# Two steps of the second phase's weight preparation on GpSimd instead of VectorE

## The chip, the cores and the metric

The kernel runs on one core of one Trainium2 chip. Its time is the device time of one execution in microseconds (us), as the median over several executions. A core has five engines that each work through their own list of instructions in order and wait for each other by semaphores: TensorE (PE in the profile; PEld is its weight load), VectorE (DVE), ScalarE (ACT), GpSimd (POOL) and SyncE (SP), which here only issues transfers (DMA).

## The reference

Three parts follow each other, all in float32:

```
attention, per batch (8) and head (8):   x 512x64, state 32x64
  xread = softmax(x state^T / 8) state            512 rows
  sread = softmax(state x^T / 8) x                 32 rows
  y0 = [xread; sread] of all heads                544 x 512 per batch
first phase, per batch:
  h = relu(y0 w_in)                               512 -> 1024
  c = conv_w[0] h[s-1] + conv_w[1] h[s] + conv_w[2] h[s+1]
  y = (h * sigmoid(c)) w_out                      1024 -> 512
second phase, per batch, y1 the row before:
  xk = mu_k y + (1 - mu_k) y1     xr = mu_r y + (1 - mu_r) y1
  out = sigmoid(xr w_r) * (relu(xk w_k)^2 w_v)
```

w_in, w_out, w_k, w_v and w_r are given as 64-bit floats; the kernel gets their bits as two 32-bit words each.

## The kernel before, in words

**Products.** Matrices are kept as a high and a low part in a format of float32 that TensorE takes; `mm3` (lines 111 to 117) makes a product from three: high by high (line 115), high by low (116) and low by high (117). So nearly every operand needs two steps: a copy to the high part (`hi`, ScalarE) and a subtraction that gives the low part (`lo`, mostly VectorE).

**Weights.** `Weights` (lines 120 to 170) loads and converts a chunk of 128x1024 weights. `load` puts the 64-bit words into a buffer `raw`; `split` makes float32 values and their two parts: ScalarE takes the low words' absolute value into `mid` (line 161) and scales the high words (163); VectorE sets the sign (164), clamps `mid` between two constants (165) and joins both (166); ScalarE copies the high part out (168) and VectorE subtracts (169). `raw` and `mid` have two buffers each (line 20), shared in turn by all chunks, so a chunk's load waits for the low part (169) of the chunk two before it. The second phase has ten chunks: four of w_k, four of w_v and two of w_r.

**Phases.** The first phase goes through nine tiles t: one per batch with 512 tokens (0 to 7; the attention of the next batch runs beside them) and one with the state rows of all batches. Each tile has eight blocks f of 128 inner columns. A block is a product `hps` on TensorE, then `hb` (relu, ScalarE, line 452), `cacc` (the convolution: one step on ScalarE, 468, two on VectorE, 470), `g` (sigmoid on ScalarE, 478, a product on VectorE, 479), `gs` (high part on ScalarE, 485, low part, 487, on GpSimd for tiles 0 to 2 and on VectorE for the others), and the products `acc` of `gs` with w_out, which sum over the blocks. After a tile `yo` goes to memory. GpSimd fills the two border columns of each `hb` (451) and copies two columns to `carry` (453). The second phase loads `y` again as `yt`, forms `mix` and `xk`, `xr` from it (557 to 565), and has blocks of its own: `kps`, `k`, `k2`, `ks`, sums `acc` with w_v, and `rps` with w_r.

**Order.** The code gives every piece of work a priority by its block (lines 750 to 795); the pieces that prepare weights get theirs from `weight_at` (725), some blocks before they are needed. The framework then lays the instructions of each engine into one fixed list by these priorities and by the durations that its own planner assumes. On the chip each engine keeps that list: a step that waits holds back everything behind it on its engine. The first w_k chunk is converted near the end of tile 6 of the first phase.

Of the kernel before, what the change touches and what calls it, by code (L numbers as in the profile page):

```python
# [8 lines left out]
F32 = mybir.dt.float32  # L9
# [3 lines left out]
ALU = mybir.AluOpType  # L13
# [19 lines left out]
def tile_kernel(  # L33
# [26 lines left out]
    nc = tc.nc  # L60
# [11 lines left out]
    N = 512  # L72
# [10 lines left out]
    wp = ctx.enter_context(tc.tile_pool(name="wp", bufs=1))  # L83
    stg = ctx.enter_context(tc.tile_pool(name="stg", bufs=2))
# [3 lines left out]
    op = ctx.enter_context(tc.tile_pool(name="op", bufs=1))  # L88
# [31 lines left out]
    class Weights:  # L120

        def __init__(self, src, many, n, pool, tag="", home=None):
            self.src, self.many, self.n, self.pool, self.tag, self.home = src, many, n, pool, tag, home
            self.wide = src[0].dtype != F32

# [17 lines left out]
        def split(self, w, first=0):  # L145

            hi, lo = w[:, 0], w[:, 1]
            if not self.wide:
                nc.scalar.activation(hi, self.raw, AF.Copy)
                nc.vector.tensor_tensor(lo, self.raw, hi.bitcast(F32), op=ALU.subtract)
                return
            many = w.shape[2]
            raw = self.raw[:, first:first + many]
            v, e = raw[:, :, :, 0], raw[:, :, :, 1]
            x = self.tile([P, many, self.n], U32, "mid")
            vf, ef, xf = v.bitcast(F32), e.bitcast(F32), x.bitcast(F32)  # L160
            nc.scalar.activation(xf, ef, AF.Abs, scale=2.0**16)
            most = float.fromhex("0x1.dffffep+32")
            nc.scalar.activation(v, v, AF.Copy, scale=0.936 * 2.0**-29)
            nc.vector.scalar_tensor_tensor(v, e, 0x80000000, v, op0=ALU.bitwise_and, op1=ALU.bitwise_or)
            nc.vector.tensor_scalar(xf, xf, scalar1=2.0, scalar2=most, op0=ALU.max, op1=ALU.min)
            nc.vector.scalar_tensor_tensor(v, x, 3, v, op0=ALU.logical_shift_left, op1=ALU.bitwise_or)
            return (
                nc.scalar.activation(hi, vf, AF.Copy),
                nc.vector.tensor_tensor(lo, vf, hi.bitcast(F32), op=ALU.subtract),
            )  # L170

    W = {}
# [2 lines left out]

        return tc.issue_after(i.ins)

    def weight(src, key, tag, pool, k, many, group, home=None):


        r = Weights([src[k + i] for i in range(many)], many, N, stg, home=home)

        def split(first=0, n=many):
            g = (key, "group", k // group)
            if k % group == 0 and first == 0:
                W[g] = pool.tile([P, 2, group, N], F32R, tag=f"{tag}{k // group}", name=f"{key}{k}")
            o = k % group + first
            for i in range(n):
                W[key, k + first + i] = W[g][:, :, o + i]
            return r.split(W[g][:, :, o:o + n], first)  # L190

        return r.load, split
# [332 lines left out]
    def load_y(t, pool):  # L525
        q0, ss = tok_segs(t)
        n = ss[-1][2] + ss[-1][1]
        y = pool.tile([P, KC, N + 2], F32, tag="yt", name="yt", bufs=1)
        o = 0
        while o < n:  # L530
            b, s = divmod(q0 + o, T + 1)
            s -= 1
            if s < 0:
                m = 1
                nc.gpsimd.memset(y[:, :, o:o + 1], 0.0)
            elif s < S - 1:
                m = min(n - o, S - 1 - s)
                nc.sync.dma_start(out=y[:, :, o:o + m], in_=y_d[b][:, :, s:s + m])
            else:
                m = min(n - o, T - s)  # L540
                c = b * E + s - (S - 1)
                nc.sync.dma_start(out=y[:, :, o:o + m], in_=y_d[B][:, :, c:c + m])
            o += m
        yt[t] = y
# [84 lines left out]
    def at_half(k, *fns, prio=None):  # L629
        p = 500 * k - AHEAD if prio is None else prio  # L630
        half.setdefault(k, []).extend((fn, p) for fn in fns)

    def run_half(k):
        for fn, p in half.pop(k, []):
            tc.cur_priority = BASE + p
            fn()
# [88 lines left out]
    def weight_at(w, need, at):  # L725
        at_half(at, w[0], w[1], prio=500 * need - WEIGHT_AHEAD)
# [22 lines left out]
    p2 = None  # L749
    for i in range(len(slots) + 2):  # L750
        if i < len(slots):
            ph, t, f = slots[i]
            if (ph, t, f) == (1, B - 1, 2):
                ap_cm.__exit__(None, None, None)
                p2 = ctx.enter_context(tc.tile_pool(name="p2", bufs=1))
                for k in range(0, KF, 2):
                    w = weight(w_k, "k", "wk", p2, k, 2, 2)
                    h = h2 + 2 * k
                    weight_at(w, h, h - 4)
                for k in range(0, KF, 2):  # L760
                    w = weight(w_v, "v", "wa", wp, k, 2, 4)
                    h = h2 + 2 * k + 4
                    weight_at(w, h + 1, h - 3)
                for k in range(0, KC, 2):
                    w = weight(w_r, "r", "wb", wp, k, 2, 2)
                    h = h2 + 8
                    weight_at(w, h, h - 2)
                at_half(2 * i + 4, lambda: load_y(0, p2))
                for c in range(KC):
                    at_half(h2 - 7 + 2 * c, lambda c=c: mix(0, 0, c, p2))  # L770
                    at_half(h2 + 2 + c, lambda c=c: mix(0, 1, c, p2))
            if ph == 2:
                if f == 2 and t + 1 < NT2:
                    at_half(2 * i + 2, lambda t=t: load_y(t + 1, p2))
                    for c in range(KC):
                        at_half(2 * i + 4 + 2 * c, lambda t=t, c=c: mix(t + 1, 0, c, p2))
                if f == 0 and t:
                    for c in range(KC):
                        at_half(2 * i + c, lambda t=t, c=c: mix(t, 1, c, p2))
                if f >= 4 and f - 4 < W2[t] // P:  # L780
                    at_half(2 * i, lambda t=t, f=f: g2_r(t, f - 4))

        def emit(k, d):
            if 0 <= i - d < len(slots):
                ph, t, f = slots[i - d]
                tc.cur_priority = BASE + 1000 * (i - d) + STAGE[k]
                FN[ph][k](t, f)

        emit(0, 0)
        emit(3, 2)  # L790
        emit(2, 1)
        emit(1, 0)
        run_half(2 * i)
        emit(4, 2)
        run_half(2 * i + 1)
# [55 lines left out]
```

## Time and profile before

| | us |
|---|---|
| median of 3 executions | 886.2 (883.36 to 887.11) |
| profiled execution, its own time | 881.77 |
| its span, first to last instruction | 879.9 |
| TensorE busy | 853.5 (97%) |
| VectorE busy | 546.4 (62%) |
| ScalarE busy | 545.6 (62%) |
| GpSimd busy | 105.4 (12%) |
| mean granted TensorE clock | 0.984 of full speed |

The shares are means over stages that differ much. A row of a timeline has the start from the beginning of the span, the duration, the engine, the line of the kernel, the operation, what it writes and reads, and in brackets how long the engine was idle before it and what ended that. Duration and start of neighbouring rows overlap a little, since an engine begins a step before the last one has left it.

### The profile page before, as it was taken

Reading aid. Unit: us, or ns where it says so; the run is one execution under the profiler, and the core shown is the slowest. Engines: PE = TensorE matmul, PEld = TensorE weight load, DVE = VectorE, ACT = ScalarE, POOL = GpSimd, SP = SyncE. Lnnn points to the kernel's source line nnn. Section 1 sums busy time; section 2 is a strip of 40 time slices with the busy share of each in tenths; the row PEclk is TensorE's granted clock in tenths of the full one; section 3 lists DMA queues with packets and bytes.
Section 4 is the critical chain, followed back from the end, with each engine's and each line's share of the span. In section 5 each row is a group of like instructions: output and inputs, shape, how many; then the busy total and the mean of one; then the engine's idle time right before and its main releaser. Section 6 shows DMA issues by size and latency. Waiting matters only on the chain.

```text
span 879.9 us, 11844 instructions
## 1 busy us (share of the span) xinstructions
PE 853.5 (97%) x4406; PEld 686.2 (78%) x4406; DVE 546.4 (62%) x908; ACT 545.6 (62%) x952; POOL 105.4 (12%) x215
## 2 busy tenths in 40 slices
PE   5989999999999997999999999999999999999997
PEld 2557787788778775899888888888888888888886
DVE  6899987899799879999645533425334253332311
ACT  6787875787578658888756645636356364553421
POOL 1144543422111111210000000000000000000000
PEclk7899999999999998999999999999999999999999
DMA  9351254525534364233210211011100111001010
GB/s 340 116 197 49 102 143 128 150 75 160 156 114 121 96 197 151 96 144 120 98 48 37 49 48 31 17 48 49 48 23 26 49 48 48 19 18 48 1 48 36
DMA packets 45512, 76.85 MB, mean 87 GB/s; under 512 B 8336, under 2 KB 30352, under 8 KB 43408
## 3 DMA queue, kind: packets, MB, share of 16 engines
q1 hardware_dynamic: 45456, 76.12, 26.6%
q8 instruction: 34, 0.56, 0.3%
q14 instruction: 22, 0.18, 0.1%
HBM read 45.66 MB, written 17.86 MB: 72 GB/s over the span
## 4 chain that ended last, share of the span: by engine, by line
PE 88%; DVE 5%; ACT 3%; DMA 2%; SPq 1%; issue 1%; DVEq 0%; ACTq 0%
PE acc L115 14%; PE acc L116 14%; PE acc L117 14%; PE kps L115 7%; PE kps L116 7%; PE kps L117 7%; PE rps L117 4%; PE rps L116 4%; PE rps L115 4%; PE hps L115 3%; PE hps L117 3%; PE hps L116 3%; PE p_s L297 2%; PE p_m L116 1%; PE p_m L117 1%; SPq L248 1%
## 5 line engine op out<-in xcount | busy, mean ns | idle before, releaser
L594 DVE TENSOR_TENSOR ks<-k,ks 128x512 fp32r<-128x512 f32 (+1 forms) x72 | 47.6, 662 | 119.8 <-ACT ks L593 119.2
L116 PE MATMUL kps<-xk,k 128*128 128x512 f32 (+1 forms) x288 | 110.1, 382 | 0.0
L115 PE MATMUL kps<-xk,k 128*128 128x512 f32 (+1 forms) x288 | 110.1, 383 | 0.0
L117 PE MATMUL kps<-xk,k 128*128 128x512 f32 (+1 forms) x288 | 110.0, 382 | 0.0
L116 PE MATMUL acc<-gs,out 128*128 128x512 f32 (+1 forms) x288 | 109.6, 382 | 0.0
L117 PE MATMUL acc<-gs,out 128*128 128x512 f32 (+1 forms) x288 | 109.1, 380 | 0.0
L115 PE MATMUL acc<-v,ks 128*128 128x512 f32 x272 | 106.7, 392 | 0.0
L116 PE MATMUL acc<-v,ks 128*128 128x512 f32 x272 | 105.9, 389 | 0.0
L117 PE MATMUL acc<-v,ks 128*128 128x512 f32 x272 | 105.8, 392 | 0.0
L470 DVE SCALAR_TENSOR_TENSOR cacc<-hb,vcol,cacc 128x512 f32<-128x512 f32 (+1 forms) x138 | 103.3, 759 | 3.2 <-ACT cacc L468 2.7
L115 PE MATMUL acc<-gs,out 128*128 128x512 f32 (+1 forms) x288 | 95.0, 391 | 5.8 <-ACT gs L485 5.8
L559 DVE SCALAR_TENSOR_TENSOR mix<-yt,muc,mix 128x384 f32<-128x384 f32 (+7 forms) x128 | 61.4, 500 | 47.0 <-ACT mix L557 46.2
L593 ACT ACTIVATE ks<-k 128x512 fp32r<-128x512 f32 (+1 forms) x72 | 43.5, 605 | 71.2 <-PE acc L117 71.0
L557 ACT ACTIVATE mix<-yt,om 128x384 f32<-128x384 f32 (+7 forms) x128 | 61.5, 516 | 33.0 <-DMA yt<-y 16.2
L580 ACT ACTIVATE k<-kps 128x512 f32<-128x512 f32 (+1 forms) x72 | 40.9, 569 | 50.4 <-PE kps L117 50.0
L115 PEld LDWEIGHTS acc<-gs,out 128*128 128x128 f32 x288 | 54.0, 192 | 18.3 <-ACT gs L485 7.3
L116 PEld LDWEIGHTS acc<-gs,out 128*128 128x128 f32 x288 | 54.2, 188 | 13.1 <-issue 2.5
L565 DVE TENSOR_TENSOR xr<-mix,xr 128x512 fp32r<-128x512 f32 (+1 forms) x36 | 23.8, 661 | 62.8 <-ACT xr L564 62.8
L117 PEld LDWEIGHTS acc<-gs,out 128*128 128x128 f32 x288 | 54.2, 188 | 10.6 <-issue 0.8
L116 PEld LDWEIGHTS kps<-xk,k 128*128 128x128 f32 x288 | 54.4, 189 | 10.4
L117 PEld LDWEIGHTS kps<-xk,k 128*128 128x128 f32 x288 | 54.3, 188 | 10.2
L115 PEld LDWEIGHTS kps<-xk,k 128*128 128x128 f32 x288 | 54.2, 188 | 10.2
(138 smaller groups left out, 1762.1 us busy)
## 6 DMA issues: line engine op xcount, KB each, us to landing
out<-r SPq DMA_DIRECT2D x34, 256.0 KB, 2.0
xT<-x_t SPq DMA_DIRECT2D x32, 256.0 KB, 4.0
xn<-x_n SPq DMA_DIRECT2D x8, 1024.0 KB, 4.9
y<-yo SPq DMA_DIRECT2D x8, 1024.0 KB, 4.3
me<-m SPq DMA_DIRECT2D x48, 128.0 KB, 2.4
m_odd<-m SPq DMA_DIRECT2D x48, 128.0 KB, 2.4
raw<-w_out SPq DMA_DIRECT2D x8, 512.0 KB, 4.7
raw<-w_k SPq DMA_DIRECT2D x8, 512.0 KB, 4.5
```

The source lines that it names most:

```text
L115: nc.tensor.matmul(ps, lh, rh, start=start and k == 0, stop=False)
L116: nc.tensor.matmul(ps, lh, rl, start=False, stop=False)
L117: nc.tensor.matmul(ps, ll, rh, start=False, stop=stop and k == last)
L248: nc.sync.dma_start(out=m_of(b + j, q)[ri, :, g].bitcast(F32), in_=r[rj, :, i].bitcast(F32))
L297: nc.tensor.matmul(self.v["s", g][NS * j:NS * (j + 1), :], sT[self.b][r, h // 2, h % 2], xT[self.b][r, h // 2], start=True, stop=True,)
L470: nc.vector.scalar_tensor_tensor(a[:, :n], hb[:, k:k + n], w[k], a[:, :n], op0=ALU.mult, op1=ALU.add)
L557: nc.scalar.activation(tmp[:, o:o + m], y[:, c, q - 1:q - 1 + m], AF.Copy, scale=om[:, i:i + 1])
L559: nc.vector.scalar_tensor_tensor(tmp[:, o:o + m], y[:, c, q:q + m], muc[:, i:i + 1], tmp[:, o:o + m], op0=ALU.mult, op1=ALU.add,)
L565: nc.vector.tensor_tensor(dst[t][:, 1, c, :n], tmp[:, :n], hi.bitcast(F32), op=ALU.subtract)
L580: nc.scalar.activation(k[:, :n], s["p"][:, :n], AF.Relu)
L593: nc.scalar.activation(ks[:, 0, :n], s["k2"][:, :n], AF.Copy)
L594: nc.vector.tensor_tensor(ks[:, 1, :n], s["k2"][:, :n], ks[:, 0, :n].bitcast(F32), op=ALU.subtract)
```

## The change

For the ten chunks of the second phase, the clamp of `mid` and the subtraction for the low part are issued on GpSimd; the chunks of the first phase keep them on VectorE. `Weights` gets the engine as an argument, and `weight` hands it on. Sizes, buffers, priorities and the arithmetic are as they were. In the changed kernel all lines from 125 on have a number one higher.

```diff
--- before.py
+++ after.py
@@ -121,7 +121,8 @@
 
 
 
-        def __init__(self, src, many, n, pool, tag="", home=None):
+        def __init__(self, src, many, n, pool, tag="", home=None, helper=None):
+            self.helper = helper or nc.vector
             self.src, self.many, self.n, self.pool, self.tag, self.home = src, many, n, pool, tag, home
             self.wide = src[0].dtype != F32
 
@@ -162,11 +163,11 @@
             most = float.fromhex("0x1.dffffep+32")
             nc.scalar.activation(v, v, AF.Copy, scale=0.936 * 2.0**-29)
             nc.vector.scalar_tensor_tensor(v, e, 0x80000000, v, op0=ALU.bitwise_and, op1=ALU.bitwise_or)
-            nc.vector.tensor_scalar(xf, xf, scalar1=2.0, scalar2=most, op0=ALU.max, op1=ALU.min)
+            self.helper.tensor_scalar(xf, xf, scalar1=2.0, scalar2=most, op0=ALU.max, op1=ALU.min)
             nc.vector.scalar_tensor_tensor(v, x, 3, v, op0=ALU.logical_shift_left, op1=ALU.bitwise_or)
             return (
                 nc.scalar.activation(hi, vf, AF.Copy),
-                nc.vector.tensor_tensor(lo, vf, hi.bitcast(F32), op=ALU.subtract),
+                self.helper.tensor_tensor(lo, vf, hi.bitcast(F32), op=ALU.subtract),
             )
 
     W = {}
@@ -175,10 +176,10 @@
 
         return tc.issue_after(i.ins)
 
-    def weight(src, key, tag, pool, k, many, group, home=None):
-
-
-        r = Weights([src[k + i] for i in range(many)], many, N, stg, home=home)
+    def weight(src, key, tag, pool, k, many, group, **how):
+
+
+        r = Weights([src[k + i] for i in range(many)], many, N, stg, **how)
 
         def split(first=0, n=many):
             g = (key, "group", k // group)
@@ -754,15 +755,15 @@
                 ap_cm.__exit__(None, None, None)
                 p2 = ctx.enter_context(tc.tile_pool(name="p2", bufs=1))
                 for k in range(0, KF, 2):
-                    w = weight(w_k, "k", "wk", p2, k, 2, 2)
+                    w = weight(w_k, "k", "wk", p2, k, 2, 2, helper=nc.gpsimd)
                     h = h2 + 2 * k
                     weight_at(w, h, h - 4)
                 for k in range(0, KF, 2):
-                    w = weight(w_v, "v", "wa", wp, k, 2, 4)
+                    w = weight(w_v, "v", "wa", wp, k, 2, 4, helper=nc.gpsimd)
                     h = h2 + 2 * k + 4
                     weight_at(w, h + 1, h - 3)
                 for k in range(0, KC, 2):
-                    w = weight(w_r, "r", "wb", wp, k, 2, 2)
+                    w = weight(w_r, "r", "wb", wp, k, 2, 2, helper=nc.gpsimd)
                     h = h2 + 8
                     weight_at(w, h, h - 2)
                 at_half(2 * i + 4, lambda: load_y(0, p2))
```

The framework orders all engines anew. On ScalarE, at the end of tile 6 (`hb_3361` is block 6 of that tile, `gs_3355` its block 4, `k0_4040` the first chunk of w_k, `mid_4135` and `raw_4131` the second), there stood:

```order
L452 ACTIVATE hb_3361<-hps_3348 128x512
L168 ACTIVATE k0_4040<-raw_4037 128x1024
L478 ACT_TABLE_LOAD
L478 ACTIVATE g_3321<-cacc_3259 128x512
L478 ACTIVATE g_3358<-cacc_3328 128x512
L468 ACTIVATE cacc_3365<-hb_3361,vcol_97 128x512
L161 ACTIVATE mid_4135<-raw_4131 128x1024
L163 ACTIVATE raw_4131<-raw_4131 128x1024
L485 ACTIVATE gs_3355<-g_3321 128x512
```

and there stands now:

```order
L453 ACTIVATE hb_3361<-hps_3348 128x512
L479 ACT_TABLE_LOAD
L479 ACTIVATE g_3321<-cacc_3259 128x512
L469 ACTIVATE cacc_3365<-hb_3361,vcol_97 128x512
L479 ACTIVATE g_3358<-cacc_3328 128x512
L169 ACTIVATE k0_4040<-raw_4037 128x1024
L162 ACTIVATE mid_4135<-raw_4131 128x1024
L164 ACTIVATE raw_4131<-raw_4131 128x1024
L486 ACTIVATE gs_3355<-g_3321 128x512
```

The first chunk's high part has moved from the front of the table load to behind the second `g`; the same eight steps stand between `hb_3361` and `gs_3355`.

On VectorE, at tile 6's last two blocks (`gs_3481` and `gs_3514`; `raw_4131` and `raw_4155` are the second w_k chunk and the first w_v chunk), there stood:

```order
L169 TENSOR_TENSOR k2_4134<-raw_4131,k2_4134 128x1024
L470 SCALAR_TENSOR_TENSOR cacc_3491<-hb_3487,vcol_97,cacc_3491 128x512
L166 SCALAR_TENSOR_TENSOR raw_4155<-mid_4159,raw_4155 128x1024
L487 TENSOR_TENSOR gs_3481<-g_3407,gs_3481 128x512
L479 TENSOR_TENSOR g_3484<-g_3484,hb_3410 128x512
L470 SCALAR_TENSOR_TENSOR cacc_3491<-hb_3487,vcol_97,cacc_3491 128x512
L470 SCALAR_TENSOR_TENSOR cacc_3524<-hb_3520,vcol_97,cacc_3524 128x512
L487 TENSOR_TENSOR gs_3514<-g_3484,gs_3514 128x512
```

and there stands now:

```order
L480 TENSOR_TENSOR g_3407<-g_3407,hb_3361 128x512
L471 SCALAR_TENSOR_TENSOR cacc_3414<-hb_3410,vcol_97,cacc_3414 128x512
L167 SCALAR_TENSOR_TENSOR raw_4131<-mid_4135,raw_4131 128x1024
L488 TENSOR_TENSOR gs_3481<-g_3407,gs_3481 128x512
L165 SCALAR_TENSOR_TENSOR raw_4155<-raw_4155 128x1024
L471 SCALAR_TENSOR_TENSOR cacc_3491<-hb_3487,vcol_97,cacc_3491 128x512
L480 TENSOR_TENSOR g_3484<-g_3484,hb_3410 128x512
L471 SCALAR_TENSOR_TENSOR cacc_3491<-hb_3487,vcol_97,cacc_3491 128x512
L167 SCALAR_TENSOR_TENSOR raw_4155<-mid_4159,raw_4155 128x1024
L471 SCALAR_TENSOR_TENSOR cacc_3524<-hb_3520,vcol_97,cacc_3524 128x512
L488 TENSOR_TENSOR gs_3514<-g_3484,gs_3514 128x512
```

The second w_k chunk's low part (`k2_4134`) is gone from here, and the step of the w_v chunk that reads `mid_4159` has moved from ahead of `gs_3481` to behind it, two places ahead of `gs_3514`.

On GpSimd, over the same stretch, there stood:

```order
L535 MEMSET yt_3641 128x4
L451 MEMSET hb_3410 128x2
L451 MEMSET hb_3487 128x2
L453 COPY carry_100<-hb_3410 128x2
L453 COPY carry_100<-hb_3487 128x2
L451 MEMSET hb_3520 128x2
L453 COPY carry_100<-hb_3520 128x2
L451 MEMSET hb_3563 128x2
```

and there stands now:

```order
L536 MEMSET yt_3641 128x4
L452 MEMSET hb_3410 128x2
L170 TENSOR_TENSOR k0_4040<-raw_4037,k0_4040 128x1024
L166 TENSOR_SCALAR mid_4135<-mid_4135 128x1024
L452 MEMSET hb_3487 128x2
L454 COPY carry_100<-hb_3410 128x2
L452 MEMSET hb_3520 128x2
L454 COPY carry_100<-hb_3487 128x2
L166 TENSOR_SCALAR mid_4159<-mid_4159 128x1024
L454 COPY carry_100<-hb_3520 128x2
L170 TENSOR_TENSOR k2_4134<-raw_4131,k2_4134 128x1024
L452 MEMSET hb_3563 128x2
```

Three clamps (`mid_4135`, `mid_4159` and, further up, the first chunk's) and two low parts (`k0_4040`, `k2_4134`) stand between the fills and copies of `hb`.

On TensorE, at the products of tile 6's last block, there stood:

```order
L115 MATMUL acc0_3181<-gs_3514,out6_716 128x512
L115 MATMUL acc1_3182<-gs_3514,out6_716 128x512
L115 MATMUL acc2_3183<-gs_3514,out6_716 128x512
L115 MATMUL acc3_3184<-gs_3514,out6_716 128x512
L115 MATMUL hps_3620<-aring_102,m_odd_554 128x512
L116 MATMUL hps_3620<-aring_102,m_odd_554 128x512
L117 MATMUL hps_3620<-aring_102,m_odd_554 128x512
L115 MATMUL hps_3620<-aring_102,m_odd_554 128x512
L116 MATMUL hps_3620<-aring_102,m_odd_554 128x512
L117 MATMUL hps_3620<-aring_102,m_odd_554 128x512
L116 MATMUL acc0_3181<-gs_3514,out6_716 128x512
```

and there stands now:

```order
L115 MATMUL acc0_3181<-gs_3514,out6_716 128x512
L115 MATMUL acc1_3182<-gs_3514,out6_716 128x512
L115 MATMUL acc2_3183<-gs_3514,out6_716 128x512
L115 MATMUL acc3_3184<-gs_3514,out6_716 128x512
L116 MATMUL acc0_3181<-gs_3514,out6_716 128x512
L117 MATMUL acc0_3181<-gs_3514,out6_716 128x512
```

The block `hps_3620` of the next tile has moved from between the high products and the low ones to a place behind them all.

## Rows read from the trace of the kernel before

**Rows 1.** Windows: length; busy PE, PEld, DVE, ACT, POOL; clock, DMA share, GB/s.
```profile
80.00:120.00 40.00, 39.91 (x204) 32.10 (x202) 37.97 (x59) 30.03 (x52) 23.82 (x33) 1.00 0.30 99
320.00:340.00 20.00, 12.73 (x109) 9.36 (x108) 17.10 (x26) 17.38 (x25) 2.87 (x8) 0.84 0.68 211
340.00:420.00 80.00, 80.00 (x451) 71.89 (x450) 77.09 (x121) 67.56 (x120) 11.44 (x31) 1.00 0.34 122
420.00:880.00 460.00, 455.27 (x2009) 375.71 (x2007) 171.51 (x294) 231.04 (x427) 0.63 (x6) 1.00 0.12 38
```

**Rows 2.** TensorE's waits: us in total, times, longest us.
```profile
PE acc L115 <- ACT gs L485: 5.8, 2, 5.6
```

**Rows 3.** TensorE's timeline, tile 6 to 7: start, us, line, operation [idle before].
```profile
335.91 2.07 PE L115 MATMUL acc<-gs,out 128*128 128x512 f32 x4 [5.56 <-ACT gs L485]
...
340.34 0.52 PE L115 MATMUL hps<-aring,m_odd 128*128 128x512 f32 x1
...
343.70 1.07 PE L115 MATMUL acc<-gs,out 128*128 128x512 f32 x4
```

**Rows 4.** ScalarE's timeline from the last `hb` before the gap.
```profile
328.03 0.60 ACT L452 ACTIVATE hb<-hps 128x512 f32<-128x512 f32 x1 [2.09 <-PE hps L117]
329.08 1.13 ACT L168 ACTIVATE k<-raw 128x1024 fp32r<-128x1024 f32 x1 [0.45 <-PE p_srT L396]
```

**Rows 5.** VectorE's groups by shape, 340 to 420: count, busy us, mean ns.
```profile
L470 DVE SCALAR_TENSOR_TENSOR cacc<-hb,vcol,cacc 128x512 f32<-128x512 f32 x18 | 13.2, 745 | 0.0
...
L479 DVE TENSOR_TENSOR g<-g,hb 128x512 f32<-128x512 f32 x10 | 6.8, 684 | 0.0
L165 DVE TENSOR_SCALAR mid<-mid 128x1024 f32<-128x1024 f32 x7 | 4.8, 691 | 0.2 <-ACT mid L161 0.2
...
L169 DVE TENSOR_TENSOR k<-raw,k 128x1024 fp32r<-128x1024 f32 x3 | 3.7, 1217 | 0.0
```

**Rows 6.** Lines 487 and 227 on GpSimd: count, shortest/median/longest ns.
```profile
L487 POOL TENSOR_TENSOR gs<-g,gs x24: 1277/1363/1793, 35.9 to 174.2; 128x512 fp32r<-128x512 f32 x24
...
L227 POOL TENSOR_TENSOR aux<-sT,aux x6: 733/831/1717, 69.3 to 181.7; 128x256 fp32r<-128x256 f32 x6
```

**Rows 7.** GpSimd's groups by shape, whole execution.
```profile
L652 POOL MEMSET aux<- 128x2048 f32 x1 | 1.8, 1805 | 0.0
...
L306 POOL MEMSET s<- 128x1 f32 x8 | 0.7, 100 | 7.2 <-DVE sr L387 7.2
masks.py:199 POOL TENSOR_SCALAR_AFFINE_SELECT ident<-ident 128x128 f32<-128x128 f32 x1 | 0.3, 292 | 0.0
```

**Rows 8.** Timelines of VectorE and GpSimd, first tiles.
```profile
79.70 1.78 DVE L470 SCALAR_TENSOR_TENSOR cacc<-hb,vcol,cacc 128x512 f32<-128x512 f32 x1
...
79.26 1.67 POOL L487 TENSOR_TENSOR gs<-g,gs 128x512 fp32r<-128x512 f32 x1 [0.52 <-ACT gs L485]
```

**Rows 9.** VectorE's groups by shape, 80 to 120.
```profile
L470 DVE SCALAR_TENSOR_TENSOR cacc<-hb,vcol,cacc 128x512 f32<-128x512 f32 x17 | 16.3, 969 | 0.6 <-ACT cacc L468 0.4
L479 DVE TENSOR_TENSOR g<-g,hb 128x512 f32<-128x512 f32 x8 | 7.1, 890 | 0.1
```

**Rows 10.** Timelines of VectorE and TensorE, tile 6's last block.
```profile
348.75 0.68 DVE L487 TENSOR_TENSOR gs<-g,gs 128x512 fp32r<-128x512 f32 x1
...
350.50 1.07 PE L115 MATMUL acc<-gs,out 128*128 128x512 f32 x4
...
352.77 0.39 PE L116 MATMUL acc<-gs,out 128*128 128x512 f32 x1
```

**Rows 11.** DMA issues: count, KB each, median us from issue to landing.
```profile
raw<-w_v SPq DMA_DIRECT2D x8, 512.0 KB, 4.6
```

**Rows 12.** Timelines of SyncE's queue, VectorE and TensorE, start of phase two.
```profile
414.36 1.24 SPq L538 DMA_DIRECT2D yt<-y  x2
...
415.34 1.22 DVE L169 TENSOR_TENSOR k<-raw,k 128x1024 fp32r<-128x1024 f32 x1
...
423.37 0.34 PE L117 MATMUL kps<-xk,k 128*128 128x384 f32 x1
```

## Prediction

> **What bounds the kernel now.** The windows by stage come first [rows 1]. From 340 us on TensorE is busy in every microsecond (80.00 of 80, then 455.27 of 460, the rest being the tail), so nothing that another engine saves there can shorten the kernel; another engine can only make TensorE wait. The second view is TensorE's own waits [rows 2]: the longest that the change can touch is 5.6 us on `gs`, made by ScalarE's line 485. In TensorE's timeline it ends at 335.91 [rows 3], near the end of tile 6 of the first phase, exactly where the first weights of the second phase are converted. The fourth view is ScalarE's timeline there [rows 4]: after `hb` at 328.03 it runs the first `k` (329.08) and then a table load, two `g`, a `cacc` and the second chunk's `mid` and `raw` before the `gs` for which TensorE stands still. Last, VectorE between 340 and 420 us: 77.09 us busy in 80 [rows 1]. So TensorE bounds the stretch, with VectorE just behind it.
>
> After that wait TensorE also ran slowly: the granted clock was 0.84 in 320 to 340 [rows 1], four matmuls took 2.07 us at 335.91 and 1.07 us at 343.70, and the slow row ends at 340.34 [rows 3]. That is 1.2 for 2.4 GHz over 4.4 us, so 2.2 us lost. The hole and its slow exit are worth 5.6 + 2.2 = 7.8 us, the most that can be won.
>
> **What the change moves between VectorE and GpSimd.** There are ten chunks of 128x1024. Each takes a clamp of 0.69 us and a low part of 1.22 us from VectorE. Between 340 and 420 that is 7 clamps, 4.8 us, and 8 lows (three of `k`, three of `v` and two of `r`), 9.8 us: 14.6 us off [rows 5].
>
> GpSimd shows neither operation at this size. The low: the same subtraction takes at least 1.28 us there for 128x512 and at least 0.73 for 128x256 [rows 6], so 0.55 us per 256 columns and 1.28 + 1.10 = 2.4 us for 1024 (bounds: 2.3, and 2.7 as twice the median of 1.36). The clamp reads one operand. Bounds: 0.9 us, half the 1.8 us of a fill of 2048 columns that reads nothing, and 2.4 us, as a low. The nearest row is the select of 128 columns, which reads one operand: 0.29 us; less the 0.1 of the smallest fill, 1.5 ns a column, so 1.6 us, which I take [rows 7]. In the stretch GpSimd gains 7 x 1.6 + 8 x 2.4 = 30.4 us.
>
> This is not free for VectorE. At 79.26 a `gs` low began on GpSimd and ended at 80.93; the VectorE step that began at 79.70 took 1.78 us [rows 8] where its kind takes 0.74 [rows 5], and ended 0.55 us after GpSimd did. Over 80 to 120 the same two kinds averaged 969 and 890 ns [rows 9], against 745 and 684 where GpSimd has no such work [rows 5]: 17 x 0.224 + 8 x 0.206 = 5.5 us lost beside 23.8 us of GpSimd [rows 1], 23%. These kinds, with two operands in SBUF, filled 45% of that window. After the change nearly all VectorE work in 340 to 420 is of that sort: (77.1 - 14.6) / 80 = 78%. Scaled, 23% becomes 40%, or 12 us of the 30.4. Net: 14.6 off, 12 back, 2.4 us of relief; bounds 30.4 x 0.23 = 7.0 back (7.6 of relief) and all 30.4 back (15.8 worse). VectorE is hardly relieved, though the new order leans on it as if it were.
>
> The Trainium skill, "SBUF — State Buffer", section "SBUF: two separate sides", speaks against the change: VectorE and GpSimd lock the port pair that they share for a whole instruction, and the loser blocks fully, a VectorE step with two SBUF inputs included when the GpSimd step reads SBUF. The pair of rows agrees. By it all the time that falls over such steps is lost; that is the third rival, priced there from rows.
>
> **The first hole.** ScalarE has the same eight steps between `hb` and `gs`; only the first `k` moves behind the two `g`. In the trace `k` waited 0.45 us before 329.08 [rows 4]; later, it waits no more, provided the clamp and VectorE's step after it are done by 332 (a clamp from 323.3 to 325, then about 4 us of queued VectorE work). So the hole shrinks by 0.45 us; bounds 0 and 7.8 won. `hb` at 328.03 waits for transfers and matmuls that are not moved.
>
> **The place where TensorE will wait.** Tile 6's last block. Its low part ran at 348.75 and TensorE used it at 352.77, after the four high products at 350.50 and a block of `hps` between [rows 10]. The new order has no `hps` there: the low is wanted at about 351.4. On VectorE it now stands behind the step on line 167 that waits for GpSimd's clamp of the first `v` chunk. By hand: the first `k` low runs on GpSimd from 333 to 335.5 and frees the raw buffer, so `v` loads from 335.6, lands 4.6 us later [rows 11], and its `mid` ends at 341.4. The second chunk's clamp has held GpSimd until 342; two small copies and the `v` clamp then get in between VectorE's steps until about 348. Line 167 ends near 350, and the second `k` low, ready since 345, takes 2.4 us about then. One `cacc` and the block's low follow: ready at about 353.7, 2.3 us late. Behind the waiting step stand the next tile's `cacc` and `g`, and behind those ScalarE's `gs`.
>
> The Trainium skill, "GPSIMD Engine Reference", section "Engine selection", has one-input work on GpSimd at roughly line rate; at the 1.2 GHz of its table the clamp would take about 0.9 us, an estimate. Two clamps stand in this place, so it would cost 2.3 - 2 x 0.7 = 0.9 us, and the sum below would be 3.5. No row here shows the operation.
>
> Three more places are alike: the third `k` low (2.4 for 1.2), the two first `v` lows in a row (4.8 for 2.4), and the two `r` lows (4.8 for 2.4). They hold VectorE 1.2 + 2.4 + 2.4 = 6.0 us longer. Of this I count half: TensorE's lead of 3.3 us at 348.75 [rows 10] would hide any one of them, the 1.9 us that is left of it without the `hps` would not hide two.
>
> Sum: -0.45 + 2.3 + 3.0 = +4.9. After 440 nothing is changed: TensorE is full and its matmuls are the same. The profiled execution took 881.77 (span 879.9 and 1.9 around it), so 886.7 now; it lay 4.4 us under the median of 886.2, so **891 us**. Its own range, by the bounds of clamp and lock, is +1 to +11: 887 to 897.
>
> **The rivals.** *Hidden anyway.* In 80 to 120 TensorE was busy 39.91 of 40 us beside 23.8 us of GpSimd [rows 1], so the lock need not reach it; against it, VectorE then had half its work in forms that do not wait. Only the 0.45 remains: 881.3, on the median 886.
>
> *The hole goes.* If `gs` could pass the weights, up to 7.8 us: 874.0, or 878. ScalarE's order speaks against it: `k`, `mid` and `raw` still stand ahead.
>
> *Full lock.* Every GpSimd microsecond over a two-operand step is lost: 30.4 x 0.78 = 23.7, less 14.6, is 9.1; VectorE had 2.9 free, so 6.2 us reach TensorE: 888.0, or 892. It lies inside the forecast's range, and its chance is part of the forecast's.
>
> *The last `k` chunk comes late (slower still).* Its low began at 415.34, was there at 416.56, and TensorE used it at 423.37 [rows 12]: 6.8 us in hand. Each load waits for the low two chunks ahead, now 1 to 3 us later; and the third `v` chunk's second half now loads behind two `yt` transfers, while ScalarE takes that chunk's `mid` and `raw` before this `k`. If `yt` goes out as late as 414.36 for 1.24 us [rows 12]: 415.6, 4.6 to land, 3 x 1.1 on ScalarE, 2.4 for the low make 425.9, so 2.5 us late, and with clamps and contention up to 8. It decides once `yt` goes out after about 412. With the forecast's 4.9: 889 to 895 own, 894 to 899.
>
> **How the numbers follow.** Forecast 0.52 (0.12 of it by the full lock), hidden 0.26, the hole goes 0.10, late last chunk 0.12. A measurement here can tell 0.5%, 4.4 us, from no change; so slower begins at 890.6. Of the forecast 0.30 lie above it; with 0.12, slower is 0.42. Same is 0.22 + 0.26 = 0.48, faster 0.10. The range 882 to 899 leaves out the vanished hole and the far ends of the late cases.
>
> **What would show it.** Right: a TensorE wait of 1 to 3 us near 351 on `gs` from line 488, and more between 355 and 425; VectorE's `cacc` steps above 0.8 us on average in 340 to 420; lows near 2.4 and clamps near 1.6 us on GpSimd; the hole near 330 still at 5 us or more; `v` loading at about 335.6. Wrong: TensorE busy throughout 340 to 420 (hidden), the first hole under 2 us, or the long wait on `k` or `r` after 405.

## The result and the profile after

Four runs each: 895.06 us (892.41 to 897.27) after, 886.21 us (883.36 to 887.11) before. The ratio is 1.0113, with a 95% interval of 1.0081 to 1.0145, so the change made the kernel 0.8 to 1.5% slower. The forecast was 891 us, the range 882 to 899.

The profiled execution took 895.52 us with a span of 893.7, against 881.77 and 879.9. These 13.8 us are 8.1 us more in which TensorE was idle (893.7 - 859.2 busy, against 879.9 - 853.5) and 5.7 us more in which it was busy with the same matmuls, most of it at a lower clock. Not all of this is the change's. Up to about 320 us the two kernels have the same order on all engines, and still the later execution was behind there. This is the last step before the orders part on VectorE, first in the kernel before, then in the changed one:

```profile
321.73 1.23 DVE L164 SCALAR_TENSOR_TENSOR raw<-raw 128x1024 uint32<-128x1024 uint32 x1 [0.34 <-DMA m_odd<-m]
```

```profile
324.74 1.23 DVE L165 SCALAR_TENSOR_TENSOR raw<-raw 128x1024 uint32<-128x1024 uint32 x1 [0.32 <-DMA m_odd<-m]
```

The later execution is 3.0 us behind. So 13.8 - 3.0 = 10.8 us lie behind 320 us, beside the 8.85 between the medians. Two windows behind it, as [rows 1]:

```profile
320.00:340.00 20.00, 12.95 (x118) 9.72 (x117) 13.80 (x21) 15.24 (x23) 8.74 (x8) 0.93 0.61 172
340.00:420.00 80.00, 76.01 (x400) 66.62 (x399) 77.17 (x104) 60.32 (x108) 53.95 (x46) 0.95 0.30 109
```

The row for 340 to 420 tells most of it. GpSimd went from 11.44 to 53.95 us busy and VectorE, which gave work away, is busy 77.17 us where it was 77.09. TensorE, busy in all 80 us before, has gaps of 4 us, and its clock fell. Its waits in 320 to 460, as [rows 2]:

```profile
PE acc L115 <- DVE yo L505: 5.3, 2, 3.2
PE acc L115 <- ACT gs L486: 5.1, 1, 5.1
PE hps L115 <- DMA me<-m: 1.9, 1, 1.9
PE acc L116 <- DVE gs L488: 0.5, 1, 0.5
PE kps L115 <- ACT k L581: 0.3, 1, 0.3
```

and where they end in its timeline, as [rows 3]:

```profile
338.84 2.07 PE L115 MATMUL acc<-gs,out 128*128 128x512 f32 x4 [5.07 <-ACT gs L486]
...
355.21 0.50 PE L116 MATMUL acc<-gs,out 128*128 128x512 f32 x1 [0.50 <-DVE gs L488]
...
398.00 0.40 PE L115 MATMUL acc<-gs,out 128*128 128x272 f32 x1 [3.24 <-DVE yo L505]
...
436.71 0.79 PE L115 MATMUL acc<-v,ks 128*128 128x512 f32 x1 [2.05 <-DVE yo L505]
```

The old hole is still there, 5.07 us for 5.56. New are 0.50 + 3.24 + 0.34 + 2.05 = 6.1 us, of which 5.3 are waits for `yo`: at the end of an output tile VectorE copies every second accumulator out of PSUM, and TensorE can't start the next sum in it before. Net 5.6 us of idle time. The granted clock adds to it. It was at its lower level, 1.2 of 2.4 GHz, about the end of the hole in both kernels, and in the changed one also about the end of each of the two waits for `yo`. First the kernel before, then the changed one, the clock is the third number from the right:

```profile
333.00:341.00 8.00, 5.09 (x13) 4.04 (x14) 7.80 (x12) 8.00 (x13) 1.36 (x4) 0.57 0.35 138
```

```profile
337.00:345.00 8.00, 6.16 (x16) 4.89 (x17) 7.05 (x11) 5.70 (x11) 7.76 (x6) 0.57 0.50 176
398.00:403.00 5.00, 5.00 (x28) 5.00 (x28) 4.96 (x10) 4.61 (x9) 1.96 (x3) 0.66 0.76 302
436.00:440.00 4.00, 3.29 (x9) 2.77 (x10) 2.80 (x4) 1.83 (x3) 2.42 (x1) 0.57 0.64 217
```

The 0.43 of 8 us, 0.34 of 5 and 0.43 of 4 that are missing make 6.8 us, against 0.43 of 8 = 3.4 before, so 3.4 more. 5.6 + 3.4 are 9.0 of the 10.8. Of the rest 0.3 is a longer wait for the last transfer of `me`; 1.5 us are not assigned.

Why the copies came late is seen where two lows stand back to back on GpSimd. GpSimd's row first, then VectorE's:

```profile
390.72 5.04 POOL L170 TENSOR_TENSOR v<-raw,v 128x1024 fp32r<-128x1024 f32 x2 [1.28 <-ACT v L169]
```

```profile
392.03 1.46 DVE L480 TENSOR_TENSOR g<-g,hb 128x286 f32<-128x286 f32 x1 [1.76 <-ACT g L479]
393.42 2.66 DVE L471 SCALAR_TENSOR_TENSOR cacc<-hb,vcol,cacc 128x286 f32<-128x286 f32 x1
396.00 0.54 DVE L566 TENSOR_TENSOR xk<-mix,xk 128x384 fp32r<-128x384 f32 x1
396.47 0.50 DVE L471 SCALAR_TENSOR_TENSOR cacc<-hb,vcol,cacc 128x286 f32<-128x286 f32 x1
396.90 0.44 DVE L488 TENSOR_TENSOR gs<-g,gs 128x286 fp32r<-128x286 f32 x1
397.26 0.68 DVE L505 COPY yo<-acc 128x512 f32<-128x512 f32 x1
```

The first low ends near 393.2, the second at 395.76. The `g` step of 0.45 us took 1.46 and ended just behind the first, the `cacc` step of 0.50 took 2.66 and ended 0.3 us behind the second; between the two VectorE got in one step. The copy could have run from about 392, when TensorE had ended the last product of its sum, and stood behind them until 397.26. With their own durations the same steps in the same order would have let it end near 394.8, an estimate from the rows; TensorE stood still from 394.76 on. So the two lows make this wait. The 1.76 us in which VectorE was idle before, for a `g` of ScalarE, had used up the slack.

The other wait has the same form; GpSimd's row, then VectorE's:

```profile
432.81 2.42 POOL L170 TENSOR_TENSOR k<-raw,k 128x1024 fp32r<-128x1024 f32 x1
```

```profile
432.88 3.42 DVE L167 SCALAR_TENSOR_TENSOR raw<-mid,raw 128x1024 uint32<-128x1024 uint32 x1 [0.74 <-POOL mid L166]
```

The join took 3.42 us for 1.22, and the copy of `yo` started at 436.23. With its own 1.22 the copy would have ended near 434.5, an estimate again; TensorE stood still from 434.66. The clamp has a part in it: the join had waited 0.74 us for `mid`, and without that it would have begun ahead of the low.

VectorE's groups in 340 to 420, as [rows 5]:

```profile
L471 DVE SCALAR_TENSOR_TENSOR cacc<-hb,vcol,cacc 128x512 f32<-128x512 f32 x18 | 17.5, 983 | 0.0
L471 DVE SCALAR_TENSOR_TENSOR cacc<-hb,vcol,cacc 128x286 f32<-128x286 f32 x16 | 13.9, 873 | 0.1
L165 DVE SCALAR_TENSOR_TENSOR raw<-raw 128x1024 uint32<-128x1024 uint32 x6 | 9.2, 1540 | 1.5 <-ACT raw L164 1.5
...
L566 DVE TENSOR_TENSOR xr<-mix,xr 128x384 fp32r<-128x384 f32 x3 | 3.8, 1266 | 0.0
```

In the kernel before, the first took 745 ns [rows 5] and the others:

```profile
L164 DVE SCALAR_TENSOR_TENSOR raw<-raw 128x1024 uint32<-128x1024 uint32 x7 | 8.6, 1225 | 1.2 <-ACT raw L163 1.2
L470 DVE SCALAR_TENSOR_TENSOR cacc<-hb,vcol,cacc 128x286 f32<-128x286 f32 x16 | 8.2, 511 | 0.0
...
L565 DVE TENSOR_TENSOR xr<-mix,xr 128x384 fp32r<-128x384 f32 x4 | 2.2, 552 | 0.0
```

Against these durations the four lost 4.3 + 5.8 + 1.9 + 2.1 = 14.1 us. Taken step by step over all groups, by what ran on GpSimd beside each, VectorE lost 15.8 us: 11.9 in six steps beside the lows, which held GpSimd for 16.6 us of this window, and 3.9 in six steps beside the clamps, which held it for 22.9. And on GpSimd, 320 to 460:

```profile
L166 POOL TENSOR_SCALAR mid<-mid 128x1024 f32<-128x1024 f32 x10 | 38.3, 3829 | 20.3 <-ACT mid L162 20.3
L170 POOL TENSOR_TENSOR k<-raw,k 128x1024 fp32r<-128x1024 f32 x4 | 11.7, 2921 | 2.0 <-ACT k L169 2.0
```

A clamp costs 3.6 us or more there, where 0.69 was enough on VectorE; a low 2.4 to 3.4.

### The profile page after: what moved, and what is told of

It reads as the page before. It is cut to its first block, busy times and chain, and to the rows that moved or that the text cites. A ratio compares the mean times of both kernels' runs of the same rounds, so it can differ in the third digit from the quotient of the medians.

```text
span 893.7 us, 11858 instructions
## 1 busy us (share of the span) xinstructions
PE 859.2 (96%) x4406; PEld 689.6 (77%) x4406; DVE 550.8 (62%) x888; ACT 546.2 (61%) x952; POOL 171.4 (19%) x235
## 4 chain that ended last, share of the span: by engine, by line
PE 77%; DVE 11%; ACT 4%; DMA 3%; issue 3%; SPq 1%; POOL 1%; DVEq 0%; POOLq 0%; ACTq 0%
PE acc L115 12%; PE acc L116 12%; PE acc L117 12%; PE kps L115 7%; PE kps L117 7%; PE kps L116 7%; PE rps L117 3%; PE rps L116 3%; PE rps L115 3%; DVE cacc L471 3%; PE hps L115 2%; PE hps L117 2%; PE hps L116 2%; PE p_s L298 2%; DMA me<-m 1%
## 5 line engine op out<-in xcount | busy, mean ns | idle before, releaser
L471 DVE SCALAR_TENSOR_TENSOR cacc<-hb,vcol,cacc 128x512 f32<-128x512 f32 (+1 forms) x138 | 113.2, 831 | 5.1 <-ACT cacc L469 4.4
L116 PE MATMUL acc<-gs,out 128*128 128x512 f32 (+1 forms) x288 | 110.7, 384 | 0.5 <-DVE gs L488 0.5
L117 PE MATMUL acc<-gs,out 128*128 128x512 f32 (+1 forms) x288 | 109.8, 381 | 0.0
L115 PE MATMUL acc<-gs,out 128*128 128x512 f32 (+1 forms) x288 | 100.9, 394 | 8.5 <-ACT gs L486 5.1
L115 PEld LDWEIGHTS acc<-gs,out 128*128 128x128 f32 x288 | 55.2, 194 | 21.2 <-ACT gs L486 6.5
L116 PEld LDWEIGHTS acc<-gs,out 128*128 128x128 f32 x288 | 54.8, 190 | 14.1 <-issue 2.5
L117 PEld LDWEIGHTS acc<-gs,out 128*128 128x128 f32 x288 | 54.6, 190 | 10.6 <-issue 0.8
L115 PEld LDWEIGHTS acc<-v,ks 128*128 128x128 f32 x272 | 51.3, 189 | 13.0 <-DVE yo L505 2.5
```

Of the source, the lines that this page charges most:

```text
L115: nc.tensor.matmul(ps, lh, rh, start=start and k == 0, stop=False)
L116: nc.tensor.matmul(ps, lh, rl, start=False, stop=False)
L117: nc.tensor.matmul(ps, ll, rh, start=False, stop=stop and k == last)
L471: nc.vector.scalar_tensor_tensor(a[:, :n], hb[:, k:k + n], w[k], a[:, :n], op0=ALU.mult, op1=ALU.add)
```

## The experiments

Theory: the low on GpSimd reads two operands from SBUF, and while it runs VectorE can't start a step of its own kind; VectorE's list, which was full, falls behind, and with it the copies that free the accumulators. Rivals: the price of the clamp, 3.6 us for 0.7; lateness, GpSimd's results come too late for those who use them; and the order, which the framework made anew. Each kernel is compared with executions of the kernel before on the same chip.

**One half at a time.** The kernel before: 884.37 us here.

```diff
-                self.helper.tensor_tensor(lo, vf, hi.bitcast(F32), op=ALU.subtract),
+                nc.vector.tensor_tensor(lo, vf, hi.bitcast(F32), op=ALU.subtract),
```

> Only the ten clamps on GpSimd, the ten low parts back on VectorE. Theory (the low parts shut VectorE out: a VectorE step with two operands in SBUF that starts under a low on GpSimd waits to its end and then takes its full time; the clamps, with one operand, do not): the waits of TensorE for the copies of yo (3.2 and 2.0 us) are gone, no cacc step of 286 columns above 0.8 us in 380 to 420, clamps still 3.6 us; time within 4 us of before, 883 to 890. Rival one (the price of the clamp: 3.6 us on GpSimd where 0.7 was, holding the join behind it and all of VectorE's list): most of the loss stays, 891 to 896, with VectorE idle at the join. Rival two (the new order of the instructions, whichever engine does them): an order of its own, so somewhere between, with waits at other places.

885.88 us, ratio 1.0012 (0.9998 to 1.0026). TensorE's only waits from 320 to 460 are those of the kernel before, on `gs` (5.0) and `me`; VectorE's `cacc` of 286 columns averages 557 ns in 340 to 420; one of them, beside a clamp, took 1.29 us, against the expectation. The clamps cost even 4.1 us each:

```profile
L166 POOL TENSOR_SCALAR mid<-mid 128x1024 f32<-128x1024 f32 x10 | 41.4, 4143 | 29.8 <-ACT mid L162 29.7
```

So a clamp that is five times dearer does little harm by itself, against rival one.

```diff
-            self.helper.tensor_scalar(xf, xf, scalar1=2.0, scalar2=most, op0=ALU.max, op1=ALU.min)
+            nc.vector.tensor_scalar(xf, xf, scalar1=2.0, scalar2=most, op0=ALU.max, op1=ALU.min)
```

> Only the ten low parts on GpSimd, the ten clamps back on VectorE. Theory (low parts shut VectorE out): VectorE steps of two operands that start under a low still take 1.5 to 3 us, single waits of TensorE of 1 to 3 us between 355 and 440 stay, 890 to 896. Rival one (price of the clamp): the loss is gone, 884 to 889. Rival two (order): between.

892.09 us, ratio 1.0084 (1.0062 to 1.0105): most of the loss is in the lows. VectorE's `cacc` steps in 340 to 420 are nearly as slow as in the changed kernel (986 and 781 ns, for 983 and 873). The waits stand at other places, because the order is another:

```profile
PE acc L115 <- ACT gs L486: 5.6, 1, 5.6
PE kps L115 <- ACT k L581: 2.7, 2, 2.0
PE hps L115 <- DMA me<-m: 1.9, 1, 1.9
PE hps L115 <- ACT hb L453: 1.1, 2, 1.0
PE rps L116 <- POOL r L170: 0.5, 1, 0.5
PE acc L115 <- DVE yo L505: 0.4, 1, 0.4
PE hps L115 <- ACT hb L459: 0.2, 1, 0.2
```

Here 4.9 us of new waits are spread over five kinds. The halves add up to 1.2 + 8.4 = 9.6 thousandths, against 11.3 for the whole.

**A low without its second operand.** The first try of this and of the next edit had a fault: the lines also applied to the weights of the first phase.

```diff
-                self.helper.tensor_tensor(lo, vf, hi.bitcast(F32), op=ALU.subtract),
+                self.helper.tensor_scalar(lo, vf, scalar1=2.0, scalar2=most, op0=ALU.max, op1=ALU.min),
```

> Clamps on GpSimd as in the changed kernel, and in place of each low part a clamp of the same 1024 columns on GpSimd, which reads one operand (the weights' lower parts are left out, so the output lacks them). GpSimd then works longer, about 3.6 us for 2.4. Theory (lock by two operands): VectorE's cacc, gs and xr steps fall back to their own 0.5 to 0.75 us, the waits for yo are gone, 883 to 889 although GpSimd's results come 1.2 us later each. Rival one (GpSimd's results come too late): worse than the changed kernel, 896 to 902. Rival two (order): 888 to 896.

895.89 us, ratio 1.0125 (1.0106 to 1.0144). By itself that speaks for lateness or order, but TensorE already waited 6.0 us on `gs` near 60 us and came to the last `me` at 337.09 where the changed kernel was at 328.15: the loss lay ahead of the stretch in question. The same edit for the second phase alone, against 884.51 us before:

```diff
+            if self.helper is nc.gpsimd:
+                return (
+                    nc.scalar.activation(hi, vf, AF.Copy),
+                    nc.gpsimd.tensor_scalar(lo, vf, scalar1=2.0, scalar2=most, op0=ALU.max, op1=ALU.min),
+                )
```

> The same question as in the run with a one-operand step in place of the low parts, which had by mistake changed the weights of the first phase as well and so came to the last attention block 8.9 us late (337.09 for 328.15 us). Here the second phase's weights alone: clamps on GpSimd, and in place of each of their low parts a clamp on GpSimd (the lower parts are left out). Theory (the low, with two operands in SBUF, shuts VectorE out; the clamp does not): from that block on the earlier run needed 557.0 us, the changed kernel 565.5 and the kernel before 552.8, so 885 to 889 now. Rival one (GpSimd's results are late, 3.6 us for each of both steps): 894 to 899. Rival two (the order): 890 to 895.

885.10 us, ratio 1.0007 (0.9989 to 1.0024). GpSimd works more than in the changed kernel:

```profile
340.00:420.00 80.00, 79.49 (x433) 70.41 (x433) 71.32 (x110) 65.46 (x118) 61.64 (x47) 0.98 0.36 127
```

61.64 us of GpSimd beside 53.95, yet TensorE is busy 79.49 of 80 us, waits for `yo` nowhere, and VectorE has fallen to 71.32. For lateness this is no clean test: the clamp in the low's place does not read ScalarE's high part and so need not wait for it. In the last five chunks it ended 3.8 to 4.1 us behind the join, the low of the changed kernel 3.7 to 8.4. What speaks against lateness is that in the changed kernel none of TensorE's waits behind 320 us ends on a step of GpSimd. The changed kernel and the three with one part altered have each an order of their own; the two with two-operand lows on GpSimd lose and the two without do not, which an order made anew would hardly sort so. That is an argument. The two waits for `yo`, worked out above in the changed kernel's own order, bear it out for 5.3 us.

**Lows in halves.** First with the same fault, then for the second phase alone.

```diff
...
+                for c in (slice(0, self.n // 2), slice(self.n // 2, self.n)):
+                    b = nc.gpsimd.tensor_tensor(
+                        lo[:, :, c], vf[:, :, c], hi[:, :, c].bitcast(F32), op=ALU.subtract)
...
```

> The changed kernel with each low part on GpSimd cut into two of 512 columns. Theory (lock): a VectorE step that is shut out gets in between the two halves, so the longest of its kind falls from 2.9 to about 1.8 us and TensorE's waits by half: 889 to 893. Rival one (price of the clamp, lateness of GpSimd's results): no better, 894 to 897, since each low part takes 0.1 to 0.2 us longer in two pieces. Rival two (order): nearly the same order, so the same time, 893 to 897.

897.34 us, ratio 1.0142 (1.0122 to 1.0161), with the first phase's lows cut too and the last `me` at 331.60 for 328.15, so this time does not answer the question.

> The changed kernel with the second phase's low parts, and these alone, in two steps of 512 columns on GpSimd. Theory (lock): VectorE loses the sum of the lows, however they are cut, as long as it always has a step to do; the longest step falls from 2.9 to about 1.8 us, but there are twice as many, so 892 to 896, close to the changed kernel. Rival (a single long block is what hurts, since TensorE's lead covers short ones): waits for yo gone, 886 to 890.

894.10 us, ratio 1.0097 (1.0072 to 1.0123). The waits for `yo` stand at the places of the changed kernel: 3.38 us at 397.03 and 0.82 at 435.81. Step by step VectorE lost 11.9 us in 340 to 420 beside the halves, as beside the whole lows: what counts is their sum, not the length of one.

**The prices by themselves.** Behind the end of the kernel before, single steps on GpSimd and groups of four on VectorE, started together:

```diff
...
+            "low": lambda: nc.gpsimd.tensor_tensor(L, a0, H.bitcast(F32), op=ALU.subtract),
+            "clamp": lambda: nc.gpsimd.tensor_scalar(X, X, scalar1=2.0, scalar2=most, op0=ALU.max, op1=ALU.min),
+            "max": lambda: nc.gpsimd.tensor_scalar_max(X, X, 2.0),
...
+            "stt": lambda: [nc.vector.scalar_tensor_tensor(
+                d[:, 512 * j:512 * j + 512], d[:, 512 * j:512 * j + 512], w, Y[:, 0], op0=ALU.mult, op1=ALU.add)
+                for j in range(4)],
...
```

> The kernel before, with a row of single steps behind its end, so that the time is some 80 us longer: on GpSimd the low of 1024 columns, the clamp, a maximum alone and a copy, each by itself; on VectorE four steps of 512 columns with two operands in SBUF, four with one; then low and clamp beside each of the two kinds, and the low beside copies out of PSUM. Theory (lock): low 2.4 and clamp 3.6 us alone; beside a low the first of the two-operand steps takes about 2.4 + 0.7 us and the others 0.74; beside a clamp all four take 0.74, and the clamp up to 1 us longer; one-operand steps and copies from PSUM go on beside the low as if it were not there. Rival (the port is shared evenly): each of the first two or three steps takes about 1.5 us and the low 3.5 to 5 us. On the clamp: if its two operations are its price, the maximum alone takes about 1.8 us; if the form is, 3.6 too.

One execution, 939.89 us with the added steps. GpSimd alone (low, clamp, maximum, copy):

```profile
883.31 2.40 POOL L816 TENSOR_TENSOR k<-pa,k 128x1024 fp32r<-128x1024 f32 x1 [168.90 <-ACT px L840]
886.82 3.62 POOL L817 TENSOR_SCALAR px<-px 128x1024 f32<-128x1024 f32 x1 [1.12 <-ACT pz L842]
891.14 2.77 POOL L818 TENSOR_SCALAR px<-px 128x1024 f32<-128x1024 f32 x1 [0.70 <-ACT pz L842]
894.53 1.04 POOL L819 COPY py<-px 128x1024 f32<-128x1024 f32 x1 [0.61 <-ACT pz L842]
```

VectorE's four steps (shortest/median/longest ns): of two operands beside a low, of one operand beside a low, copies from PSUM beside a low, and of two operands beside a clamp:

```profile
L824 DVE SCALAR_TENSOR_TENSOR pd<-pd,vcol,py x4: 737/738/2751, 903.4 to 907.4; 128x512 f32<-128x512 f32 x4
...
L827 DVE TENSOR_SCALAR pd<-py x4: 414/414/2485, 913.9 to 917.0; 128x512 f32<-128x512 f32 x4
...
L830 DVE COPY pd<-pz x4: 680/681/691, 923.0 to 924.8; 128x512 f32<-128x512 f32 x4
...
L824 DVE SCALAR_TENSOR_TENSOR pd<-pd,vcol,py x4: 741/746/1525, 909.2 to 912.0; 128x512 f32<-128x512 f32 x4
```

The step that started 0.18 us behind the low took 2.75 us for 0.74 and ended 0.54 us behind it: it lost 2.0 of the low's 2.4 us. The next three were not slowed, and the low took 2.39 us, for 2.40 alone; so the port is not shared evenly, as the rival had it. The one-operand step was shut out as well (2.49 for 0.41), which I had not expected; the copies from PSUM were not. Beside a clamp one step in four lost 0.78 us, and the clamp, which went on for 4.04 us, did not hold the others. A maximum alone takes 2.77 us, between the two values of the expectation: the second operation costs 0.85, and most of the price is there with one; a plain copy takes 1.04.

The Trainium skill, "SBUF — State Buffer", section "Who interferes with whom", has a VectorE step of two SBUF inputs, or a `tensor_scalar` in its two-port mode, wait for the whole of a GpSimd instruction that reads SBUF. For the low the rows agree; the one-operand step agrees too if it ran in that mode, which no row names. For the clamp they do not: it also reads SBUF, and the step beside it waited 0.78 us and not 3.6.

**The old hole.** The first hole was the one thing to be won, so the kernel before got another order on ScalarE: table load and first `g` ahead of `hb`, the second chunk's `mid` and `raw` behind both `gs`.

```diff
+LATE = {2: (6, 5)}
+HB = {(1, 6, 6): (6, 4)}
...
+                if (k, t, f) in HB:
+                    with behind(GB[HB[k, t, f]]):
+                        FN[ph][k](t, f)
...
+                    if k in LATE:
+                        w = w[0], lambda w=w, k=k: after_gs(LATE[k], w[1])
...
```

> The kernel before, with ScalarE's order changed at the hole near 330 us: table load and first g go ahead of hb, and the second chunk's mid and raw behind the two gs; no step changes its engine. If the hole is made by ScalarE's order, as the prediction said, TensorE's wait on gs falls from 5.6 to about 1 us and its slow exit with it: 879 to 882. Rival: hb, about 1 us later, or the loads behind the second chunk become late, and TensorE waits there: 884 to 888.

885.19 us, ratio 1.0002 (0.9983 to 1.0021). The wait on `gs` fell to 0.7 us, and one of 3.77 us on `hb` came, as the rival had it. On ScalarE:

```profile
331.55 1.12 ACT L171 ACTIVATE k<-raw 128x1024 fp32r<-128x1024 f32 x1 [2.98 <-PE p_srT L399]
332.69 1.28 ACT L481 ACT_TABLE_LOAD   x1
333.98 0.63 ACT L481 ACTIVATE g<-cacc 128x512 f32<-128x512 f32 x1
334.52 0.58 ACT L455 ACTIVATE hb<-hps 128x512 f32<-128x512 f32 x1
```

The first chunk's `k` stands ahead of the table load and waits 2.98 us for the transposes of TensorE, and `hb` with it. So `k` went behind the first `gs` too; then, without the change to `hb`, `k` and the second chunk alone (884.27 us before).

```diff
+            if hold is not None:
+                with behind(GS[hold]):
+                    a = nc.scalar.activation(hi, vf, AF.Copy)
...
```

> As the run with ScalarE's order changed at the hole, and the first chunk's k behind the first gs as well. In that run k stood ahead of the table load and waited 2.98 us for the small transposes of TensorE, so that hb came late (TensorE waited 3.77 us on hb in place of 5.6 on gs). If that was the reason, table load and g now run in ScalarE's idle time before hb, TensorE's waits on hb and gs together fall below 2 us, and the time is 879 to 882. Rival: the hole is filled by whatever comes next (k's lower part and the loads behind it late, or the copies of yo), 884 to 887.

882.71 us, ratio 0.9983 (0.9970 to 0.9996): 0.2% under the kernel before, an interval that just leaves out no change, and between the expectation and the rival. The hole near 330 is gone; TensorE is busy 17.27 of 20 us in 320 to 340, for 12.73. Later a `gs` is 2.01 us late:

```profile
332.39 0.51 PE L119 MATMUL hps<-aring,m_odd 128*128 128x512 f32 x1 [0.43 <-ACT hb L460]
335.88 0.50 PE L120 MATMUL acc<-gs,out 128*128 128x512 f32 x1 [0.62 <-DVE gs L495]
345.43 2.08 PE L119 MATMUL acc<-gs,out 128*128 128x512 f32 x4 [2.01 <-ACT gs L493]
```

In ScalarE's list the second chunk's `k` and the third's `mid` and `raw` stand ahead of it. The weights' steps moved a part of the hole on.

> The kernel before, with the first chunk's k behind the first gs and the second chunk's mid and raw behind both, and hb left ahead of table load and g. ScalarE then has 1.1 us of k and 2.2 us of mid and raw less ahead of gs: TensorE's wait on gs falls from 5.6 to about 2.5 us, the slow exit stays or shortens: 881 to 884. Rival: the time comes back behind it as in the run before, 884 to 887.

889.41 us, ratio 1.0066 (1.0049 to 1.0082), a miss: the wait on `gs` fell to 1.93 us, but 2.03 us on the next `gs` came behind it, and near 394 1.72 us for a `yo` of ScalarE. What makes that last one late I did not look for.

## Why the prediction was right, and where it was not

**The bound** was read rightly: TensorE is the limit, VectorE just behind it, and what came of the change came as waits of TensorE and as its lower clock behind them.

**The price of a low** was 2.4 us, and is: 2.40 alone.

**The price of a clamp** was 1.6 us with bounds of 0.9 and 2.4, and is 3.62, outside them. A fill and a select [rows 7] say nothing of a step with arithmetic: the copy of the same size takes 1.04, one comparison 2.77, two 3.62. The estimate from the Trainium skill's page was worse, 0.9. It mattered little, since clamps hold VectorE little (3.9 us in 340 to 420) and alone cost at most 0.3% of the time.

**The lock.** I charged 12 of 30.4 us of GpSimd, 40%, scaled from the first tiles, to both operations alike. Lows and clamps came to 39.5 us in that window and VectorE lost 15.8, again 40%, but that is luck: it lost 72% of the lows' time (11.9 of 16.6) and 17% of the clamps' (3.9 of 22.9). Six of each ran there, about 11.5 us off VectorE, so the net relief of 2.4 us was a loss of 4.3, inside the bounds. That half of VectorE's work has forms that do not wait, as the first rival says, is too much: a one-operand step waits for a low too. The rival of the full lock had the mechanism nearly right for the low and wrong for the clamp; its 6.2 us is still under the 9.0 found.

**The first hole** was to shrink by 0.45 us and shrank by 0.49. The slow stretch did not shrink: 3.4 us are missing in the windows around it in both kernels.

**The place near 351** cost 0.50 us and not 2.3. Of the two steps that I put ahead of its low part on VectorE, the join did not wait for the clamp (which ended at 350.15; the join began at 350.49, straight behind a `cacc`), but the second `k` low did hold VectorE: a `cacc` beside it took 2.93 us, and the block's low part came at 354.48 and was ready at 355.15. With the 3.0 us by which this execution was behind already, the prediction would have it at 353.7 + 3.0 = 356.7, and wanted at 354.4; TensorE wanted it at 354.7, 0.5 us ahead of 355.21.

**The three more places** were put at 3.0 us. The two `v` lows alone cost 3.24, the third `k` low and the two `r` lows nothing, though these too held VectorE for 2.2 us each. What I missed is who waits: I looked at `gs`, and it was the copy of `yo` at a tile's end, for which TensorE has no other work to go on with.

**The last `k` chunk**: the rival's 894 to 899 holds the measured time, but not for its reason. As an operand the chunk cost nothing that the waits show; its low cost 2.05 us by shutting out the join ahead of a copy of `yo`, after that join had waited for its clamp.

**Left out of the sum** was the clock. I counted it behind the old hole and put it at nothing behind the new waits, but the two for `yo` had a stretch at 1.2 GHz about their end, 3.4 us more than before. By rows, the sum of +4.9 should have been -0.5 + 0.5 + 3.2 + 0.3 + 2.1 for waits, and 3.4 for the clock, 9.0. The range of 882 to 899 holds 895 because it is wide: the place that was worked out by hand gave a fifth of its price, and the 2.05 us of the last `k` low and the clock were not in the sum.

**The signs** that came are the waits between 355 and 425, `cacc` at 983 ns, lows of 2.4 us and the hole at 5 us; `v` loaded at 339.22, which is 336.2 without the 3.0 us. The wait near 351 was too short, and the clamps too long.

How much of the 1.2 thousandths of the clamps alone is real stays open: its interval reaches to nothing.

## What to carry to other kernels

Before work goes from VectorE to GpSimd, look at what GpSimd's step does to the steps of VectorE beside it: a low, with two operands in SBUF, took 2.0 us from VectorE on average (11.9 us for six), so moving 1.22 us of its work made it busy for longer. An engine with a full list should not be relieved like that even where the other is idle. And at an in-order engine look for the step for which the bounding engine has no substitute, here the copy that frees an accumulator, and what can be put in front of it.

## What was not expected of the hardware

A VectorE step of one SBUF operand, 512 columns in 0.41 us, is shut out by a GpSimd low like a step of two (2.49 us); a copy from PSUM is not (0.68 to 0.69). A clamp on GpSimd takes 3.62 us for 1024 columns and stops VectorE for 0.78 us of that. It works the other way too: the changed kernel's second clamp, begun at 339.17 while VectorE was busy, took 4.59 us for 3.62.
